# Linear attention and a gated MLP in one kernel: the products of keys with values in column halves of the array, each group kept together

## The chip, the cores and the metric

The kernel runs on one NeuronCore of a Trainium2 chip. A core has engines with queues of their own: TensorE (PE, with its weight loads shown apart as PEld), VectorE (DVE), ScalarE (ACT), GpSimd (POOL) and SyncE (SP), which starts the DMAs here. They meet only at semaphores. The metric is the device time of one execution in microseconds.

## The reference

Inputs are q, k, v of 8 batches x 8 heads x 576 positions x 64, a feature matrix w_phi (64 x 128), and the MoE's w_in (512 x 1024), conv_w (3 x 1024) and w_out (1024 x 512), which are float64 or float32.

```python
def phi(x):
    proj = np.einsum('bhsd,df->bhsf', x, w_phi)
    proj = proj - np.max(np.abs(proj), axis=-1, keepdims=True)
    return np.concatenate([np.exp(proj), np.exp(-proj)], axis=-1)
q_p, k_p = phi(q), phi(k)
kv = np.einsum('bhsf,bhsd->bhfd', k_p, v)
z = np.sum(k_p, axis=2)
num = np.einsum('bhsf,bhfd->bhsd', q_p, kv)
den = np.einsum('bhsf,bhf->bhs', q_p, z)[..., None] + 1e-06
x = num / den                                  # heads side by side: 8 x 576 x 512
h = np.maximum(x @ w_in, 0.0)
conv_out = conv_w[0]*h[t-1] + conv_w[1]*h[t] + conv_w[2]*h[t+1]   # along the sequence
out = (h * sigmoid(conv_out)) @ w_out
```

## The kernel before

**Tiling.** Four heads make a set (`qd`, two sets a batch). Of each set the 576 positions are worked on in five groups: group 0 holds the last 64 positions of all heads (n = 1), groups 1 to 4 hold 256 columns each (n = 2). `chains` lists the groups: the keys of batch 0, then by turns a query group of batch b and a key group of batch b + 1.

**A key group** (`k_process`, from line 222): DMAs bring kT and v, GpSimd splits k into a high and a low part (`kxh`, `kxl`), TensorE projects it with three products a tile (`kp`, lines 207 to 209), VectorE takes the largest absolute value and subtracts it (`km` line 214, `ks` line 216), ScalarE takes exp of both signs (`ke`, line 242: first s = 0, the positive sign, then s = 1), and TensorE multiplies these with v into the accumulators `kv` (two banks, i = 0 and 1; line 253 for group 0, line 258 for the others). v has a column of ones, so that z comes along: 65 columns, or 130 where two head pairs stand side by side (group 0). After group 4 ScalarE copies the accumulators to `kvf` (line 269).

**A query group** (`q_process`, from line 278) is projected in the same way (`qp`, `qm`, `qs`), transposed on TensorE (`tp`, line 298), exponentiated (`qe`, line 303), and multiplied with `kvf` into `nm` (line 322). These products stand in halves of the array: 64 stationary columns at a time, a = 0 and a = 64, which write partitions 0 to 63 and 64 to 127 of the result. VectorE divides (`dn`, `rc`, `x`, lines 333 to 336).

**The MoE** works on 12 tiles of 384 positions. `x_process` transposes x (`xt`, lines 376 and 379) and splits it (`xh`, `xl`); `h_part` makes 96 products for each tile and relu (`hp` line 407, `h` line 413); `conv_process` does the convolution, the sigmoid and the gate (`c`, `gh`, `gl`); `o_part` makes another 96 (`op`, line 468) and sends them out. `weight_process` loads and converts the MoE's weights at the start, mostly on VectorE (`w_t`, lines 101 to 108).

**What sets the order.** All these processes are generators. `merge` (line 553) keeps a clock of TensorE's time and steps through the first process that can run; `pe(n, ns)` adds n products to a count and ns to the clock, `wait` and `until` say when a process can go on, and `paced` (line 514, table `PACE`) says up to how many MoE products come before attention, by the count of attention products done. What is written so is then ordered for each engine by the framework's scheduler. `lead()` (line 505) raises the priority of what stands in it, so that it can pass MoE work that was written earlier; before the change it is around loads, VectorE's and ScalarE's steps, but not around TensorE's products. Within its limits the scheduler may spread a group's products among others.

```python
            elif can_m:
                if not step(moe, "m"):
                    moe = None
```

Of the kernel before, what the change touches and what calls it, by code (L numbers as in the profile page):

```python
# [24 lines left out]
VW = D + 1  # L25
# [4 lines left out]
ISSUE = 112  # L30
# [8 lines left out]

def PE_ORDER(tc):  # L40
    return nullcontext()


@with_exitstack
def kernel(
# [13 lines left out]
    nc = tc.nc  # L59
# [96 lines left out]
    now = [0.0]  # L156
    issued = [0.0]
    ready = {}

    def pe(n, ns):  # L160
        return ("pe", n, ns)

    def wait(ns):
        return ("wait", ns * LAT)

    def until(*keys):
        return ("until", [k for k in keys if k is not None])

    def set_ready(key, ns=0):
        ready[key] = now[0] + ns * LAT  # L170
# [8 lines left out]
    def load_split(src, b, qd, g, kind):  # L179
        c0, n = group_columns(g)  # L180
        if kind == "q" and 2 * b + qd < NQ_F32:
            raw = sb.tile([P, n * P], F32, name=f"{kind}r{b}_{qd}_{g}", tag="th", bufs=3)
            nc.sync.dma_start(out=raw, in_=src[b, qd, :, c0 : c0 + n * P])
            return n, raw, None
        raw = sb.tile([P, n * P], F32, name=f"{kind}r{b}_{qd}_{g}", tag="tr", bufs=3)
        nc.sync.dma_start(out=raw, in_=src[b, qd, :, c0 : c0 + n * P])
        hi = sb.tile([P, n * P], F32R, name=f"{kind}xh{b}_{qd}_{g}", tag="th", bufs=3)
        lo = sb.tile([P, n * P], F32R, name=f"{kind}xl{b}_{qd}_{g}", tag="tl", bufs=3)
        split(raw, hi, lo, nc.gpsimd, nc.gpsimd)
        return n, hi, lo  # L190
# [28 lines left out]
    kv = {}  # L219
    kvps = {}  # L220

    def k_process(b, qd, g):
        j = (b * NQ + qd) * 5 + g

        def back(key, k):
            return (key, j - k) if j >= k else None

        yield until(back("kp", 2), back("kv", 3))
        with lead():
            n, hi, lo = load_split(kT, b, qd, g, "k")  # L230
            v0 = 16 if g == 0 else 4 * (g - 1)
            v = sb.tile([P, 4 * VW], F32, name=f"v{b}_{qd}_{g}", tag="v", bufs=3)
            nc.sync.dma_start(out=v, in_=vt[b, qd, :, v0 * VW : (v0 + 4) * VW])
        yield wait(3000)
        yield until(back("kv", 2))
        set_ready(("kp", j))
        pr = yield from project(n, hi, lo, b, qd, g, "k")
        with lead():
            e = []
            for s in range(2):  # L240
                e.append(sb.tile([P, 2 * n, F], F32, name=f"ke{b}_{qd}_{g}_{s}", tag="ke", bufs=3))
                nc.scalar.activation(out=e[s], in_=pr, func=AF.Exp, scale=1.0 - 2.0 * s)  # L242
        yield wait(3000)
        yield until(back("kv", 1))
        if g == 0:
            kvps[b, qd] = [pk.tile([P, 2, 2 * VW], F32, name=f"kv{b}_{qd}_{i}", tag=f"kv{i}") for i in range(2)]
        kp = kvps[b, qd]
        for t in range(n):
            for i in range(2):
                for s in range(2):  # L250
                    lhsT = e[s][:, 2 * t + i, :]
                    if g == 0:
                        nc.tensor.matmul(out=kp[i][:, s, :], lhsT=lhsT, rhs=v[:, 2 * i * VW : 2 * (i + 1) * VW],  # L253
                                         start=(s == 0), stop=False, skip_group_check=True)
                        yield pe(2, 220)
                    else:
                        p0 = (g - 1) // 2 * VW
                        nc.tensor.matmul(out=kp[i][:, s, p0 : p0 + VW], lhsT=lhsT,  # L258
                                         rhs=v[:, (2 * t + i) * VW : (2 * t + i + 1) * VW],
                                         start=False, stop=(g % 2 == 0 and t == 1), skip_group_check=True)  # L260
                        yield pe(2, 112)
        if g == 4:

            yield until(("num", 10 * (b - 1) - 1) if b > 1 else None)
            r = []
            with lead():
                for i in range(2):
                    kf = sb.tile([P, 2, 2 * VW], F32, name=f"kvf{b}_{qd}_{i}", tag="kvf", bufs=8)
                    nc.scalar.activation(out=kf, in_=kp[i], func=AF.Copy)
                    r.append(kf)  # L270
            kv[b, qd] = r
            set_ready(("kvq", b, qd), 1500)
        set_ready(("kv", j))
# [4 lines left out]
    def q_process(b, qd, g):  # L278
        j = 10 * b + QORDER.index((qd, g))

        def back(key, k):
            return (key, j - k) if j >= k else None

        yield until(back("qp", 2))
        with lead():
            n, hi, lo = load_split(qT, b, qd, g, "q")
        yield wait(3000)
        yield until(back("tp", 2))
        set_ready(("qp", j))
        pr = yield from project(n, hi, lo, b, qd, g, "q")  # L290
        yield wait(1700)
        yield until(back("num", 2))
        set_ready(("tp", j))

        tp = pg.tile([P, 2, n, P], F32, name=f"tp{b}_{qd}_{g}", tag="g", bufs=4)
        for t in range(n):
            for i in range(2):
                nc.tensor.transpose(out=tp[:, i, t, :], in_=pr[:, 2 * t + i, :], identity=idn)  # L298
                yield pe(1, 60)
        with lead():  # L300
            qe = sb.tile([P, 2, 2, n, P], F32, name=f"qe{b}_{qd}_{g}", tag="qe", bufs=2)
            for s in range(2):
                nc.scalar.activation(out=qe[:, s], in_=tp, func=AF.Exp, scale=1.0 - 2.0 * s)  # L303
        yield wait(2000)
        yield until(back("num", 1), ("kvq", b, qd))

        if g > 0:
            xorder.append((b, g))
            i = len(xorder) - 1 - NX
            yield until(("xc", last_chunk(*xorder[i])) if i >= 0 else None)  # L310
        else:
            yield until(("xc", last_chunk(b - 2, 0)) if b > 1 else None)


        w = 2 * VW if g == 0 else VW
        p0 = 0 if g == 0 else (g - 1) // 2
        ps = pg.tile([P, n, 2, w], F32, name=f"nm{b}_{qd}_{g}", tag="g", bufs=4)
        for t in range(n):
            for i in range(2):
                for s in range(2):  # L320
                    for a in (0, 64):
                        nc.tensor.matmul(out=ps[a : a + 64, t, i, :], lhsT=qe[:, s, i, t, a : a + 64],  # L322
                                         rhs=kv[b, qd][i][:, s, p0 * VW : p0 * VW + w],
                                         start=(s == 0), stop=(s == 1))
        yield pe(16 * n, 100)
        parts = [(0, 64, 0), (64, 128, VW)] if g == 0 else [(0, P, 0)]
        with lead():
            dn = sb.tile([P, n, 2], F32, name=f"dn{b}_{qd}_{g}", tag="dn", bufs=4)
            rc = sb.tile([P, n, 2], F32, name=f"rc{b}_{qd}_{g}", tag="rc", bufs=4)
            x = sb.tile([P, n, 2, D], F32, name=f"x{b}_{qd}_{g}", tag="x0" if g == 0 else "x", bufs=4 if g == 0 else NX)  # L330
            xs[b, qd, g] = x
            for a, z, c0 in parts:
                nc.vector.tensor_scalar(out=dn[a:z], in0=ps[a:z, :, :, c0 + D], scalar1=1e-6, scalar2=None, op0=ALU.add)
            nc.vector.reciprocal(out=rc, in_=dn)
            for a, z, c0 in parts:
                nc.vector.tensor_tensor(out=x[a:z], in0=ps[a:z, :, :, c0 : c0 + D],
                                        in1=rc[a:z].unsqueeze(3).broadcast_to([z - a, n, 2, D]), op=ALU.mult)
        set_ready(("num", j))
        set_ready(("xs", b, qd, g), 1500)
# [165 lines left out]
    def lead():  # L505

        return tc.high_priority(offset=ahead[0])
# [17 lines left out]
    def step(p, kind):  # L525

        for what, *arg in p[1]:
            if what == "pe":
                n, ns = arg

                issued[0] = max(issued[0] + ISSUE * n, now[0] - 30 * ISSUE)
                now[0] = max(now[0], issued[0]) + ns
                done[kind] += n
                p[0] = now[0]
                return True
            if what == "wait":
                p[0] = now[0] + arg[0]
                return True
            p.append(arg[0])
            return True  # L540
        return False
# [43 lines left out]
    with PE_ORDER(tc):  # L585
        merge()
# [56 lines left out]
```

## Time and profile before

| | |
|---|---|
| Median of 3 runs | 858.72 us (856.85 to 863.38) |
| The profiled execution: its time | 853.69 us |
| Its span, first to last instruction | 851.9 us |
| Mean granted TensorE clock | 0.992 |
| Busiest after TensorE | VectorE, 537.3 us |

How to read what follows. A group row gives line, engine, operation, tiles out<-in, the part of the array used (rows*columns), the shape and the count; then busy time in us, the mean time of one in ns, and the idle time of the engine just before it with what ended that. A timeline row gives start, length, engine, line, operation, tiles and how many equal ones were merged. Matmuls overlap, so that one lasts longer than the distance to the next start; the distance is what one costs in a stream. A matmul with four-byte operands is shown as two records.

### The profile page before, as it was taken

To read this page: it belongs to the slowest core of one execution; us is meant where nothing else is said; L and a number is where in the kernel's file an instruction comes from. 1 tells how busy PE (TensorE), PEld (TensorE's weight loads), DVE (VectorE), ACT (ScalarE), POOL (GpSimd) and SP (SyncE) were. 2 spreads that over 40 slices of the span, in tenths; PEclk is the share of its full clock that TensorE was granted. 3 is DMA by queue.
4 is the path that set the end of the run, shared out by engine and by line. 5 is a ranking of instruction groups with operands and counts; after the bars stand their busy time and mean duration, and the time that the engine had idled before them with its cause. 6 is when DMAs were issued, how large, how long until landed. Compare 5 with 4: busy or idle time off the path is not lost.

```text
span 851.9 us, 17963 instructions
## 1 busy us (share of the span) xinstructions
PE 820.0 (96%) x7118; PEld 780.4 (92%) x7118; DVE 537.3 (63%) x1110; ACT 389.6 (46%) x678; POOL 275.0 (32%) x434
## 2 busy tenths in 40 slices
PE   7988898999999999998999999999999999999898
PEld 7887898999999999898998999999999999999798
DVE  7989978656565737655555665675564666574541
ACT  5676546354444344345344435425435434534332
POOL 5776853323322404213212421340332343110110
PEclk9999999999999999999999999999999999999899
DMA  6553311022012112012112201201201210000001
GB/s 196 178 157 125 104 36 42 22 76 61 25 54 67 44 35 73 20 48 72 33 44 60 67 19 63 63 17 57 70 17 47 76 50 29 22 3 28 10 28 47
DMA packets 46595, 48.74 MB, mean 57 GB/s; under 512 B 5296, under 2 KB 44464, under 8 KB 46512
## 3 DMA queue, kind: packets, MB, share of 16 engines
q1 hardware_dynamic: 46512, 47.59, 18.6%
q8 instruction: 57, 0.93, 0.5%
q14 instruction: 26, 0.21, 0.1%
HBM read 38.13 MB, written 9.44 MB: 56 GB/s over the span
## 4 chain that ended last, share of the span: by engine, by line
PE 83%; DVE 10%; ACT 3%; issue 2%; DMA 1%; POOL 0%; SPq 0%; ACTq 0%; POOLq 0%; DVEq 0%
PE hp L407 23%; PE op L468 23%; PE kv L258 10%; PE nm L322 9%; PE tp L298 3%; PE xt L376 3%; PE kp L207 2%; PE qp L207 2%; PE qp L209 2%; PE qp L208 1%; PE kp L208 1%; PE kp L209 1%; PE kv L253 1%; DVE ks L216 1%; DVE km L214 1%
## 5 line engine op out<-in xcount | busy, mean ns | idle before, releaser
L434 DVE SCALAR_TENSOR_TENSOR c<-h,cw,c 128x384 f32<-128x384 f32 (+3 forms) x256 | 131.3, 545 | 77.7 <-POOL c L428 75.8
L258 PE MATMUL kv<-v,ke 128*128 128x65 f32 x1024 | 131.0, 273 | 5.5 <-ACT ke L242 5.3
L258 PEld LDWEIGHTS kv<-v,ke 128*128 128x128 f32 x1024 | 126.3, 192 | 9.8 <-ACT ke L242 7.9
L242 ACT ACTIVATE ke<-ks 128x512 f32<-128x512 f32 (+1 forms) x160 | 87.2, 584 | 105.0 <-DVE ks L216 83.4
L407 PE MATMUL hp<-xh,win_hi 128*128 128x386 f32 x384 | 132.7, 356 | 2.0 <-ACT xh L69 1.7
L407 PE MATMUL hp<-xl,win_hi 128*128 128x386 f32 x384 | 132.3, 345 | 0.0
L407 PE MATMUL hp<-xh,win_lo 128*128 128x386 f32 x384 | 130.5, 340 | 0.0
L468 PE MATMUL op<-gh,wout_hi 128*128 128x384 f32 x384 | 129.7, 339 | 0.0
L468 PE MATMUL op<-gh,wout_lo 128*128 128x384 f32 x384 | 129.0, 336 | 0.0
L468 PE MATMUL op<-gl,wout_hi 128*128 128x384 f32 x384 | 128.9, 336 | 0.0
L428 POOL TENSOR_SCALAR c<-h,cw 128x384 f32<-128x384 f32 x96 | 58.4, 610 | 172.7 <-ACT h L413 172.7
L413 ACT ACTIVATE h<-hp 128x386 f32<-128x386 f32 x96 | 46.4, 493 | 140.1 <-PE hp L407 140.0
L322 PEld LDWEIGHTS nm<-kvf,qe 128*64 128x64 f32 x2304 | 84.2, 138 | 22.9 <-issue 12.9
L322 PE MATMUL nm<-kvf,qe 128*64 128x65 f32 (+1 forms) x2304 | 101.6, 234 | 3.8 <-ACT qe L303 2.1
L71 POOL TENSOR_SCALAR kxh<-kr 128x256 fp32r<-128x256 f32 (+1 forms) x80 | 35.8, 448 | 174.7 <-PE kp L208 141.5
L303 ACT ACTIVATE qe<-tp 128x512 f32<-128x512 f32 (+1 forms) x160 | 78.2, 555 | 25.5 <-PE tp L298 25.1
L74 DVE TENSOR_TENSOR gl<-c,gh 128x768 fp32r<-128x768 f32 x48 | 45.1, 964 | 61.3 <-ACT gh L69 61.2
L71 POOL TENSOR_SCALAR qxh<-qr 128x256 fp32r<-128x256 f32 (+1 forms) x70 | 30.8, 442 | 147.4 <-PE kp L208 77.0
L407 PEld LDWEIGHTS hp<-xh,win_hi 128*128 128x128 f32 x384 | 70.5, 188 | 4.9 <-ACT xh L69 2.2
L407 PEld LDWEIGHTS hp<-xl,win_hi 128*128 128x128 f32 x384 | 73.0, 190 | 0.4 <-issue 0.2
L407 PEld LDWEIGHTS hp<-xh,win_lo 128*128 128x128 f32 x384 | 72.6, 189 | 0.3 <-issue 0.2
L214 DVE TENSOR_REDUCE km<-kp 128x4 f32<-128x512 f32 (+1 forms) x80 | 50.3, 633 | 35.4 <-PE kp L209 34.6
(68 smaller groups left out, 1504.7 us busy)
## 6 DMA issues: line engine op xcount, KB each, us to landing
v<-in_vt_dram SPq DMA_DIRECT2D x80, 130.0 KB, 2.1
kr<-in_kT_dram SPq DMA_DIRECT2D x64, 128.0 KB, 2.1
qr<-in_qT_dram SPq DMA_DIRECT2D x64, 128.0 KB, 2.1
out_dram<-os SPq DMA_DIRECT2D x32, 192.0 KB, 1.9
w_r<-in_w_in_dram SPq DMA_DIRECT2D x8, 512.0 KB, 3.6
w_r<-in_w_out_dram SPq DMA_DIRECT2D x8, 512.0 KB, 3.4
out_dram<-os SPq DMA_DIRECT2D x32, 96.0 KB, 1.7
kr<-in_kT_dram SPq DMA_DIRECT2D x16, 64.0 KB, 2.1
```

Source lines behind the costliest of these rows:

```text
L71: nc.gpsimd.tensor_scalar(out=hi, in0=src, scalar1=1.0, scalar2=0.0, op0=ALU.mult, op1=ALU.add)
L74: eng_lo.tensor_tensor(out=lo, in0=src, in1=hi.bitcast(F32), op=ALU.subtract)
L214: nc.vector.tensor_reduce(out=m, in_=ps3, axis=AX, op=ALU.max, apply_absolute_value=True)
L242: nc.scalar.activation(out=e[s], in_=pr, func=AF.Exp, scale=1.0 - 2.0 * s)
L258: nc.tensor.matmul(out=kp[i][:, s, p0 : p0 + VW], lhsT=lhsT, rhs=v[:, (2 * t + i) * VW : (2 * t + i + 1) * VW], start=False, stop=(g % 2 = ...
L303: nc.scalar.activation(out=qe[:, s], in_=tp, func=AF.Exp, scale=1.0 - 2.0 * s)
L322: nc.tensor.matmul(out=ps[a : a + 64, t, i, :], lhsT=qe[:, s, i, t, a : a + 64], rhs=kv[b, qd][i][:, s, p0 * VW : p0 * VW + w], start=(s = ...
L407: nc.tensor.matmul(out=ps, lhsT=w_, rhs=x_[:, p, :], start=(k == 0), stop=(k == 11))
L413: nc.scalar.activation(out=hs, in_=ps, func=AF.Relu)
L428: nc.gpsimd.tensor_scalar(out=cv, in0=hs[:, o : o + TC], scalar1=cw[:, f, 1:2], scalar2=0.0, op0=ALU.mult, op1=ALU.add)
L434: nc.vector.scalar_tensor_tensor(out=cv[:, lo:hi], in0=hs[:, o + j - 1 + lo : o + j - 1 + hi], scalar=cw[:, f, j : j + 1], in1=cv[:, lo:hi ...
L468: nc.tensor.matmul(out=ps, lhsT=w_, rhs=x_, start=(i == 0), stop=(i == 23))
```

## The change

Three things are changed, all on TensorE. The products of keys with values are split into column halves like those of the queries: for each of them two products with 64 stationary columns, one for partitions 0 to 63 of the accumulator and one for 64 to 127, so 1152 instead of 576. Each group's products, of keys and of queries, stand in a block with raised priority (`lead()`) and in the order in which they are written (`PE_RUN`); both begin with s = 1, the exponential that is made last, and the outermost loop of the keys' block is now over s. And the planner is told of a group as one piece: 230 + 930 n ns, with no separate issue time.

```diff
+def PE_RUN(tc):
+    return tc.manual_schedule(engines={mybir.EngineType.PE})
...
-    def pe(n, ns):
-        return ("pe", n, ns)
+    def pe(n, ns, issue=ISSUE):
+        return ("pe", n, ns, issue)
...
-        for t in range(n):
-            for i in range(2):
-                for s in range(2):
-                    lhsT = e[s][:, 2 * t + i, :]
-                    if g == 0:
-                        nc.tensor.matmul(out=kp[i][:, s, :], lhsT=lhsT, rhs=v[:, 2 * i * VW : 2 * (i + 1) * VW],
-                                         start=(s == 0), stop=False, skip_group_check=True)
-                        yield pe(2, 220)
-                    else:
-                        p0 = (g - 1) // 2 * VW
-                        nc.tensor.matmul(out=kp[i][:, s, p0 : p0 + VW], lhsT=lhsT,
...
-                        yield pe(2, 112)
+        p0 = (g - 1) // 2 * VW
+        with lead(), PE_RUN(tc):
+            for s in (1, 0):
+                for t in range(n):
+                    for i in range(2):
+                        for a in (0, 64):
+                            lhsT = e[s][:, 2 * t + i, a : a + 64]
+                            if g == 0:
+                                nc.tensor.matmul(out=kp[i][a : a + 64, s, :], lhsT=lhsT,
+                                                 rhs=v[:, 2 * i * VW : 2 * (i + 1) * VW],
+                                                 start=(s == 1), stop=False, skip_group_check=True)
+                            else:
+                                nc.tensor.matmul(out=kp[i][a : a + 64, s, p0 : p0 + VW], lhsT=lhsT,
...
+        yield pe(16 * n, 230 + 930 * n, 0)
...
-        for t in range(n):
-            for i in range(2):
-                for s in range(2):
-                    for a in (0, 64):
...
-        yield pe(16 * n, 100)
+        with lead(), PE_RUN(tc):
+            for t in range(n):
+                for i in range(2):
+                    for s in (1, 0):
+                        for a in (0, 64):
...
+        yield pe(16 * n, 230 + 930 * n, 0)
...
-                issued[0] = max(issued[0] + ISSUE * n, now[0] - 30 * ISSUE)
+                issued[0] = max(issued[0] + issue * n, now[0] - 30 * ISSUE)
```

Two places show what this does to TensorE's order. The first is the third group of keys (`v_0_2`, set 0 of batch 3) about a third into the program. Names carry the set, the group and a running number; `ke_0_2_0` and `ke_0_2_1` are the two exponentials. Before:

```order
L258 MATMUL kv_0_0_3030<-v_0_2_3066,ke_0_2_0_3202 128x65
L258 MATMUL kv_0_1_3031<-v_0_2_3066,ke_0_2_0_3202 128x65
L207 MATMUL kp_0_4_3333<-wbd_hi,kxh_0_4_3237 128x256
L208 MATMUL kp_0_4_3333<-wbd_lo,kxh_0_4_3237 128x256
L209 MATMUL kp_0_4_3333<-wbd_hi,kxl_0_4_3238 128x256
L207 MATMUL kp_0_4_3333<-wbd_hi,kxh_0_4_3237 128x256
L208 MATMUL kp_0_4_3333<-wbd_lo,kxh_0_4_3237 128x256
L258 MATMUL kv_0_0_3030<-v_0_2_3066,ke_0_2_1_3204 128x65
L258 MATMUL kv_0_1_3031<-v_0_2_3066,ke_0_2_1_3204 128x65
L258 MATMUL kv_0_0_3030<-v_0_2_3066,ke_0_2_0_3202 128x65
```

The same group on TensorE after the change, with what stands on either side of it:

```order
L304 MATMUL tp_0_4_3641<-idn,qs_0_4_3523 128x128 x4
L383 MATMUL xt_0_3717<-idn,x_0_1_3061 128x128 x2
L264 MATMUL kv_0_0_3482<-v_0_2_3475,ke_0_2_1_3564 64x65 x2
L264 MATMUL kv_0_1_3483<-v_0_2_3475,ke_0_2_1_3564 64x65 x2
L264 MATMUL kv_0_0_3482<-v_0_2_3475,ke_0_2_1_3564 64x65 x2
L264 MATMUL kv_0_1_3483<-v_0_2_3475,ke_0_2_1_3564 64x65 x2
L264 MATMUL kv_0_0_3482<-v_0_2_3475,ke_0_2_0_3562 64x65 x2
L264 MATMUL kv_0_1_3483<-v_0_2_3475,ke_0_2_0_3562 64x65 x2
L264 MATMUL kv_0_0_3482<-v_0_2_3475,ke_0_2_0_3562 64x65 x2
L264 MATMUL kv_0_1_3483<-v_0_2_3475,ke_0_2_0_3562 64x65 x2
L211 MATMUL kp_0_4_3745<-wbd_hi,kxh_0_4_3635 128x256
```

The eight whole products, before cut in two by a projection, are sixteen halves in one piece, and those that read the later exponential come first.

The second place is on TensorE too, early in the program, where two query groups (`nm_1_1` and `nm_1_3`) meet the first key group of the next batch. Before:

```order
L253 MATMUL kv_0_0_753<-v_0_0_644,ke_0_0_0_717 128x130
L322 MATMUL nm_1_1_804<-kvf_1_0_749,qe_1_1_553 64x65 x4
L322 MATMUL nm_1_3_827<-kvf_1_0_749,qe_1_3_584 64x65 x4
L298 MATMUL tp_0_2_862<-idn,qs_0_2_651 128x128 x4
L253 MATMUL kv_0_0_753<-v_0_0_644,ke_0_0_1_719 128x130
L253 MATMUL kv_0_1_754<-v_0_0_644,ke_0_0_0_717 128x130
L253 MATMUL kv_0_1_754<-v_0_0_644,ke_0_0_1_719 128x130
L322 MATMUL nm_1_1_804<-kvf_1_1_751,qe_1_1_553 64x65 x4
```

After, at the same groups:

```order
L264 MATMUL kv_1_1_556<-v_1_4_734,ke_1_4_0_814 64x65 x2
L260 MATMUL kv_0_0_873<-v_0_0_742,ke_0_0_1_828 64x130 x2
L329 MATMUL nm_1_1_931<-kvf_1_0_869,qe_1_1_629 64x65
L329 MATMUL nm_1_3_957<-kvf_1_0_869,qe_1_3_660 64x65
L329 MATMUL nm_1_1_931<-kvf_1_0_869,qe_1_1_629 64x65
L329 MATMUL nm_1_3_957<-kvf_1_0_869,qe_1_3_660 64x65
```

Two groups whose blocks are open at the same time are interleaved product by product, where four of one group stood together before; and here kv and nm, both in halves now, follow each other directly.

More of the change, by code (lines that the diff above doesn't have):

```diff
@@ L247, in k_process @@
         kp = kvps[b, qd]
-        for t in range(n):
-            for i in range(2):
-                for s in range(2):
-                    lhsT = e[s][:, 2 * t + i, :]
-                    if g == 0:
-                        nc.tensor.matmul(out=kp[i][:, s, :], lhsT=lhsT, rhs=v[:, 2 * i * VW : 2 * (i + 1) * VW],
-                                         start=(s == 0), stop=False, skip_group_check=True)
-                        yield pe(2, 220)
-                    else:
-                        p0 = (g - 1) // 2 * VW
-                        nc.tensor.matmul(out=kp[i][:, s, p0 : p0 + VW], lhsT=lhsT,
-                                         rhs=v[:, (2 * t + i) * VW : (2 * t + i + 1) * VW],
-                                         start=False, stop=(g % 2 == 0 and t == 1), skip_group_check=True)
-                        yield pe(2, 112)
+        p0 = (g - 1) // 2 * VW
[11 more added lines that the diff above has]
+                                nc.tensor.matmul(out=kp[i][a : a + 64, s, p0 : p0 + VW], lhsT=lhsT,
+                                                 rhs=v[:, (2 * t + i) * VW : (2 * t + i + 1) * VW],
+                                                 start=False, stop=(g % 2 == 0 and t == 1), skip_group_check=True)
+        yield pe(16 * n, 230 + 930 * n, 0)
         if g == 4:
@@ L317, in q_process @@
         ps = pg.tile([P, n, 2, w], F32, name=f"nm{b}_{qd}_{g}", tag="g", bufs=4)
-        for t in range(n):
-            for i in range(2):
-                for s in range(2):
-                    for a in (0, 64):
-                        nc.tensor.matmul(out=ps[a : a + 64, t, i, :], lhsT=qe[:, s, i, t, a : a + 64],
-                                         rhs=kv[b, qd][i][:, s, p0 * VW : p0 * VW + w],
-                                         start=(s == 0), stop=(s == 1))
-        yield pe(16 * n, 100)
+        with lead(), PE_RUN(tc):
[3 more added lines that the diff above has]
+                        for a in (0, 64):
+                            nc.tensor.matmul(out=ps[a : a + 64, t, i, :], lhsT=qe[:, s, i, t, a : a + 64],
+                                             rhs=kv[b, qd][i][:, s, p0 * VW : p0 * VW + w],
+                                             start=(s == 1), stop=(s == 0))
+        yield pe(16 * n, 230 + 930 * n, 0)
         parts = [(0, 64, 0), (64, 128, VW)] if g == 0 else [(0, P, 0)]
@@ L528, in step @@
             if what == "pe":
-                n, ns = arg
-                issued[0] = max(issued[0] + ISSUE * n, now[0] - 30 * ISSUE)
+                n, ns, issue = arg
+                issued[0] = max(issued[0] + issue * n, now[0] - 30 * ISSUE)
                 now[0] = max(now[0], issued[0]) + ns
```

## The prediction

> **What bounds the kernel now.** I read the page first (busy time, chain), then the busy time by stage, then the groups by form, and last the timeline of TensorE around single runs of products, since the change alters how these follow each other.
>
> ```profile
> PE 820.0 (96%) x7118; PEld 780.4 (92%) x7118; DVE 537.3 (63%) x1110; ACT 389.6 (46%) x678; POOL 275.0 (32%) x434
> PE 83%; DVE 10%; ACT 3%; issue 2%; DMA 1%; POOL 0%; SPq 0%; ACTq 0%; POOLq 0%; DVEq 0%
> ```
>
> TensorE is busy for 96% of the span and holds 83% of the chain that ended last. The page's busy time overlaps from one matmul to the next, so I price TensorE's work by the distance between starts instead. By stage (columns: length, busy time and count of PE, PEld, DVE, ACT, POOL, granted clock, DMA share, GB/s):
>
> ```profile
> 0.00:20.00 20.00, 15.77 (x102) 14.37 (x102) 13.99 (x26) 10.45 (x20) 10.91 (x23) 1.00 0.63 196
> 20.00:100.00 80.00, 70.59 (x700) 63.83 (x699) 74.79 (x135) 52.33 (x100) 60.92 (x63) 0.96 0.48 149
> 100.00:160.00 60.00, 55.53 (x494) 52.37 (x493) 48.50 (x103) 29.19 (x51) 24.63 (x37) 1.00 0.12 34
> 160.00:750.00 590.00, 583.21 (x5235) 558.70 (x5233) 355.88 (x750) 263.38 (x456) 169.04 (x297) 1.00 0.16 48
> 750.00:852.00 102.00, 94.89 (x596) 91.13 (x596) 44.14 (x99) 34.26 (x53) 9.51 (x16) 0.97 0.07 24
> ```
>
> From 20 to 100 us VectorE is the bound, at 74.8 of 80 us: it prepares the weights beside the first batches. From 160 to 750 us TensorE is, at 583.2 of 590, and VectorE has 40% to spare. A shorter TensorE is paid in full in the long stage, and hardly before 100 us.
>
> The four groups that the change touches (mean of one | idle time before):
>
> ```profile
> L258 PE MATMUL kv<-v,ke 128*128 128x65 f32 x1024 | 131.0, 273 | 5.5 <-ACT ke L242 5.3
> L253 PE MATMUL kv<-v,ke 128*128 128x130 f32 x128 | 20.2, 290 | 1.0 <-ACT ke L242 1.0
> L322 PE MATMUL nm<-kvf,qe 128*64 128x65 f32 x2048 | 82.2, 227 | 1.7 <-DVE ks L216 1.2 <-DVE dn L333 0.5
> L322 PE MATMUL nm<-kvf,qe 128*64 128x130 f32 x256 | 19.3, 291 | 2.1 <-ACT qe L303 2.1
> ```
>
> A matmul of four-byte data shows as two records here (1024 for 512 products). kv stands on the whole array (128*128), nm already in column halves (128*64), with the same 65 and 130 moving columns. So nm is the price list for the new kv.
>
> **The price of a whole-array kv record.** On the timeline, a full group of sixteen between projections, and one of the eight that are 130 wide:
>
> ```profile
> 403.07 0.28 PE L209 MATMUL qp<-wbd_hi,qxl 128*128 128x256 f32 x1
> 403.19 1.89 PE L258 MATMUL kv<-v,ke 128*128 128x65 f32 x16
> 404.90 0.36 PE L207 MATMUL kp<-wbd_hi,kxh 128*128 128x256 f32 x1
> 405.10 0.28 PE L208 MATMUL kp<-wbd_lo,kxh 128*128 128x256 f32 x1
> ...
> 409.46 1.06 PE L253 MATMUL kv<-v,ke 128*128 128x130 f32 x8
> 410.36 0.60 PE L298 MATMUL tp<-idn,qs 128*128 128x128 f32 x4
> ```
>
> The next start is 1.71 us after the first kv, and the projection behind it takes 0.20 to its successor where 0.12 is usual: 1.79 us for 16, 112 ns a record. The wide ones take 0.90 / 8, also 112 ns: doubling the columns that stream costs nothing, so streaming is not what a record waits for. The sum before is 1152 x 112 ns = 129 us.
>
> **The price of a record in halves.** Two uninterrupted nm runs between matmuls of the MoE, one of 32 records and one of 16:
>
> ```profile
> 112.68 0.33 PE L407 MATMUL hp<-xh,win_lo 128*128 128x386 f32 x1
> 112.95 1.15 PE L322 MATMUL nm<-kvf,qe 128*64 128x65 f32 x32
> 114.03 0.44 PE L407 MATMUL hp<-xh,win_hi 128*128 128x386 f32 x1
> 114.31 0.34 PE L407 MATMUL hp<-xl,win_hi 128*128 128x386 f32 x1
> 114.49 0.34 PE L407 MATMUL hp<-xh,win_lo 128*128 128x386 f32 x1
> ...
> 418.36 0.33 PE L407 MATMUL hp<-xh,win_lo 128*128 128x386 f32 x1
> 418.62 0.69 PE L322 MATMUL nm<-kvf,qe 128*64 128x65 f32 x16
> 419.24 0.44 PE L407 MATMUL hp<-xh,win_hi 128*128 128x386 f32 x1
> 419.52 0.34 PE L407 MATMUL hp<-xl,win_hi 128*128 128x386 f32 x1
> ```
>
> First nm to the next hp: 1.08 us for 32, 0.62 for 16. The difference is 29 ns a record, 0.117 us for two halves with their four records. What is left is 0.62 - 16 x 0.029 = 0.15 us for each run, whatever its length. Going in costs another 0.09 (hp to nm 0.26 to 0.27, against 0.18 from hp to hp), coming out 0.10 (0.28 against 0.18). A run of column halves thus pays about 0.34 us once. Wide and lone products:
>
> ```profile
> 400.72 1.11 PE L322 MATMUL nm<-kvf,qe 128*64 128x130 f32 x16
> 401.76 0.87 PE L376 MATMUL xt<-idn,x 128*128 128x128 f32 x6
> ...
> 163.31 0.33 PE L322 MATMUL nm<-kvf,qe 128*64 128x65 f32 x2
> 163.57 0.39 PE L209 MATMUL qp<-wbd_hi,qxl 128*128 128x256 f32 x1
> ```
>
> Wide: (1.04 - 0.15) / 16 = 56 ns a record. A lone half, with no partner, takes 0.26 - 0.15 = 0.11 us, as long as a pair: the two halves run beside each other.
>
> **The change, part by part.**
> 1. kv in halves: 2048 narrow records x 29.2 ns = 59.8 us and 256 wide x 56 = 14.3, together 74 where 129 stood: -55 us. All of it comes from the narrow ones (114.7 to 59.8); the wide ones stay at 14.3. The ends of the range are the nm price (-55) and a lone half for each product (+12, worked out at the second rival); I take the first, since shape, weights and operand sizes are those of nm.
> 2. Runs of halves: counted in the orders, 108 stretches of nm before, 126 of nm and kv after (most of 16 or 32 products). At 0.34 us, and some 0.05 less where a transpose or (before) a kv follows: 35 before, 42 after, +7 us. So keeping groups together does not save runs; it keeps kv from paying 0.34 us for each scattered pair.
> 3. Mixed runs: where two groups interleave product by product (some 230 products, the second place shown), halves follow as first, first, second, second. If each pairs with its neighbour of the other half, only the ends lose, about 4 us for all; if none pairs, 230 x 0.05 = 12. I take 3, near the first, since a half can start as soon as its own columns are free, as the lone-half row suggests.
> 4. The first 100 us:
>
> ```profile
> 0.00:100.00 100.00, 30.48 (x239) 29.09 (x239) 0.97 0.51 158
> 0.00:100.00 100.00, 5.84 (x32) 5.16 (x32) 0.97 0.51 158
> ```
>
> Of the kv records 239 narrow and 32 wide (lines 258 and 253) fall there, where VectorE is the bound. VectorE's list up to the first convolution step is as long as before (164 instructions, 159 before). Up to 239 x 53 ns = 13 us of the 55 then come out as waiting for VectorE. Its 5 idle us of 80 leave room for some, so the loss lies between 0 and 13 and I take +7.
> 5. Order inside a group (negative exponential first, at the MoE's expense): one hazard is a run that starts before its second activation is done. Waits of TensorE by releaser:
>
> ```profile
> PE kv L258 <- ACT ke L242: 5.3, 6, 1.6
> PE tp L298 <- DVE qs L216: 4.7, 6, 1.2
> PE kp L207 <- POOL kxh L71: 4.1, 1, 4.1
> ```
>
> kv waits 5.3 us in six places. Starting with the later of the two exponentials makes a group wait once, ahead of it, not within. By the prices above the new order leaves a median 5.5 us of TensorE work between a K projection and its kv (5.1 before), so I set this at 0, between -5 and +10. Behind a waiting kv on TensorE stand MoE matmuls that could have run; that is what +10 stands for.
> 6. The planner's new costs and its count of attention products (kv counts double now, so the MoE's quota opens earlier) move MoE and attention against each other by some rows in a list otherwise alike. No DMA, activation or VectorE instruction is added or removed: 0, within 5 either way.
>
> Sum: -55 + 7 + 3 + 7 = -38 us on the profiled execution's 853.69, so 816 us. That execution lies 5.0 below the median shown (858.72); three runs spread over 6.5, so I add nothing for it.
>
> **Rivals.**
>
> ```profile
> L242 ACT ACTIVATE ke<-ks 128x512 f32<-128x512 f32 (+1 forms) x160 | 87.2, 584 | 105.0 <-DVE ks L216 83.4
> ```
>
> - *TensorE gets ahead of its suppliers.* With kv at half its time, a run meets exponentials that aren't there yet. An activation of ke takes 584 ns (the row above); if half of the 80 kv groups wait that long, 23 us of the gain go: 839. Against it: 40% spare on VectorE after 160 us and the distance in part 5. It takes all 80 to give the gain back.
> - *The halves of kv do not run beside each other.* Unlike nm, kv adds to two accumulators in turn over five groups. If each half goes alone, the narrow ones take 1024 x 0.11 = 113 us (115 before) and the wide 128 x 0.223 = 28.5 (0.223 is four records of 56 ns, a lone half taking as long as a pair; 14.4 before), with +7 for the runs: 853.7 + 12 + 7 = 873, slower. The point at which it decides: a pair must take under 2 x 0.112 - 10 / 576 = 0.207 us; nm takes 0.117. The Trainium skill ("TensorE: Matmul & The Clock Gate", LDWEIGHTS) puts a weight load at columns / 1.2 ns, which is 107 ns for 128 columns and 53 for 64; that fits the 112 ns here, and if the two loads of a pair stand in line the stream would save nothing, 861 us in all. The nm rows speak against that: four loads of 64 columns pass in 117 ns where the rule in line gives 213.
> - *The start is not lost and waits shrink* (part 4 at 0, part 5 at -5): 804.
>
> **How the numbers follow.** Forecast 0.65 (its own range 804 to 828), suppliers late 0.14 (828 to 845), no pairing 0.07 (861 to 873), better than 804 0.10, slower for other reasons (the order, a clash of buffers) 0.04. The range 800 to 838 leaves out the unpaired case, the worst of the late one and the best tail, about 2 in 10. A measurement of this kernel tells 1% (8.6 us) from no change: faster 0.86, same 0.05, slower 0.09.
>
> **What would show it.** kv should appear as 128*64 with 2048 and 256 records; a lone group of 32 between MoE matmuls should last 1.08 us to the next start, a mixed run 0.47 for each 16 more. Weight preparation should still hold VectorE above 90% from 20 to 100 us, and TensorE wait more there. From 160 us the same MoE tile should come earlier and earlier, by about 5 us per batch. I am wrong if a kv group takes 1.7 us or more, if TensorE's waits for ke reach tens of us, or if the end comes after 838.

## The result

| | before | changed | ratio, 95% interval |
|---|---|---|---|
| Median of 4 runs | 857.79 us | 832.35 us | 0.970 (0.964 to 0.976) |
| The profiled execution | 853.69 us | 833.15 us | |
| Its span | 851.9 us | 831.2 us | |
| Mean granted TensorE clock | 0.992 | 0.982 | |

The change makes the kernel faster by 25 us in the medians and 20.5 between the two profiled executions; 38 were forecast for those. Two executions below, one of experiment 7 (1487 us) and the profiled one of experiment 8 (1067 us, granted clock 0.654), are slow ones and stand in no time given. The profiled execution before is the shortest of that kernel on record: the other 35 take 854.97 to 863.70 us, and the 31 of them with a clock on record have 0.976 to 0.989, median 0.984. The page after, and the stages of the changed kernel in the columns used before:

```profile
PE 780.1 (94%) x8270; PEld 731.8 (88%) x8270; DVE 545.5 (66%) x1110; ACT 385.4 (46%) x676; POOL 277.4 (33%) x434
```

```profile
20.00:100.00 80.00, 60.78 (x864) 52.05 (x863) 74.12 (x131) 48.71 (x93) 57.81 (x58) 0.91 0.49 150
100.00:160.00 60.00, 54.04 (x667) 49.68 (x668) 50.31 (x101) 33.76 (x59) 28.71 (x40) 0.97 0.15 42
160.00:750.00 590.00, 573.48 (x6158) 542.61 (x6157) 374.59 (x789) 266.94 (x467) 174.82 (x303) 0.99 0.16 48
```

VectorE still holds 93% of the stretch from 20 to 100 us, while TensorE fell from 70.6 to 60.8 busy us there. In the long stage TensorE is busy for 573.5 of 590 us; before, it was 583.2, so it now stands still for 10 us more. The groups by form and a lone group of keys, in the early part of the program:

```profile
L264 PE MATMUL kv<-v,ke 128*64 128x65 f32 x2048 | 82.1, 228 | 6.9 <-ACT ke L246 6.8
L260 PE MATMUL kv<-v,ke 128*64 128x130 f32 x256 | 21.0, 293 | 3.2 <-ACT kvf L275 2.5 <-ACT ke L246 0.7
L329 PE MATMUL nm<-kvf,qe 128*64 128x65 f32 x2048 | 87.0, 229 | 13.4 <-DVE ks L220 5.7 <-ACT qe L309 3.9 <-DVE x L343 2.7
```

```profile
41.36 0.28 PE L213 MATMUL kp<-wbd_hi,kxl 128*128 128x256 f32 x1
41.57 1.15 PE L264 MATMUL kv<-v,ke 128*64 128x65 f32 x32
42.65 0.38 PE L211 MATMUL kp<-wbd_hi,kxh 128*128 128x256 f32 x1
42.87 0.28 PE L212 MATMUL kp<-wbd_lo,kxh 128*128 128x256 f32 x1
```

Thirty-two records of kv take 42.65 - 41.57 = 1.08 us, to the hundredth what nm took before. What grew is nm's idle time, 1.7 us before and 13.4 now. Its largest releaser is VectorE's subtraction `ks`, which nm does not read at all.

**Where the time went.** To compare whole runs I split each span into TensorE's priced work (every record at its distance in an undisturbed stream: 175 ns for hp, 174 op, 118 a projection, 109 a transpose, 112 a whole kv record, 29 or 56 a half, and the steps into and out of four-byte work and runs of halves; prices times counts, so not a measurement of its own) and lost time, which is the rest and includes stretches at half clock:

| us | priced work | lost by 100 us | lost by 150 us | lost after 150 us | span |
|---|---|---|---|---|---|
| before | 798.7 | 23.8 | 29.7 | 23.5 | 851.9 |
| changed | 750.6 | 37.9 | 46.9 | 33.7 | 831.2 |
| difference | -48.1 | +14.1 | +17.2 | +10.2 | -20.7 |

The work fell as forecast (-55 + 7 + 3 = -45). That the prices hold in the changed kernel is measured on its runs of halves: 112 of the 126 are undisturbed, and from their first record to the next start they last 146.7 us together where the prices give 145.6. The lost time grew by 27 where 7 was forecast; in the medians, which differ by 25.4, that is some 23, since the profiled execution before lost less time than is usual for it. All experiments ask where those 27 us come from, and whether the 48 belong to the halves or to the order. Each ran beside the kernel before, on the same chip.

### The profile page after: what moved, and what is told of

Its sections match the earlier page's. It is cut to its first block, busy times and chain, and to the rows that moved or that the text cites. A ratio compares the mean times of both kernels' runs of the same rounds, so it can differ in the third digit from the quotient of the medians.

```text
span 831.2 us, 20238 instructions
## 1 busy us (share of the span) xinstructions
PE 780.1 (94%) x8270; PEld 731.8 (88%) x8270; DVE 545.5 (66%) x1110; ACT 385.4 (46%) x676; POOL 277.4 (33%) x434
## 3 DMA queue, kind: packets, MB, share of 16 engines
q8 instruction: 66, 1.08, 0.5%
## 4 chain that ended last, share of the span: by engine, by line
PE 67%; DVE 7%; ACT 1%; issue 0%; ACTq 0%
PE op L475 21%; PE hp L414 20%; PE nm L329 7%; PE kv L264 6%; DVE gl L78 3%; PE tp L304 3%; PE xt L383 2%; PE qp L211 2%; PE qp L213 1%; PE qp L212 1%; PE kv L260 1%; DVE km L218 1%; PE kp L211 1%; DVE qm L218 1%; PE kp L213 1%; PE kp L212 1%
## 5 line engine op out<-in xcount | busy, mean ns | idle before, releaser
L441 DVE SCALAR_TENSOR_TENSOR c<-h,cw,c 128x191 f32<-128x191 f32 (+3 forms) x256 | 133.6, 555 | 71.9 <-POOL c L435 70.2
L329 PE MATMUL nm<-kvf,qe 128*64 128x65 f32 (+1 forms) x2304 | 104.3, 235 | 14.5 <-DVE ks L220 5.7
L435 POOL TENSOR_SCALAR c<-h,cw 128x384 f32<-128x384 f32 x96 | 61.2, 639 | 158.5 <-ACT h L420 158.5
L329 PEld LDWEIGHTS nm<-kvf,qe 128*64 128x64 f32 x2304 | 91.2, 141 | 26.0 <-issue 14.1
L78 DVE TENSOR_TENSOR gl<-c,gh 128x768 fp32r<-128x768 f32 x48 | 49.2, 1047 | 67.5 <-ACT gh L73 67.4
L264 PE MATMUL kv<-v,ke 128*64 128x65 f32 x2048 | 82.1, 228 | 6.9 <-ACT ke L246 6.8
L264 PEld LDWEIGHTS kv<-v,ke 128*64 128x64 f32 x2048 | 72.9, 141 | 17.4 <-ACT ke L246 8.1
L449 DVE TENSOR_TENSOR c<-c,h 128x384 f32<-128x384 f32 x96 | 49.8, 588 | 36.1 <-ACT c L445 36.1
```

Source lines behind the costliest of these rows:

```text
L78: eng_lo.tensor_tensor(out=lo, in0=src, in1=hi.bitcast(F32), op=ALU.subtract)
L264: nc.tensor.matmul(out=kp[i][a : a + 64, s, p0 : p0 + VW], lhsT=lhsT, rhs=v[:, (2 * t + i) * VW : (2 * t + i + 1) * VW], start=False, stop ...
L435: nc.gpsimd.tensor_scalar(out=cv, in0=hs[:, o : o + TC], scalar1=cw[:, f, 1:2], scalar2=0.0, op0=ALU.mult, op1=ALU.add)
L441: nc.vector.scalar_tensor_tensor(out=cv[:, lo:hi], in0=hs[:, o + j - 1 + lo : o + j - 1 + hi], scalar=cw[:, f, j : j + 1], in1=cv[:, lo:hi ...
L449: nc.vector.tensor_tensor(out=c4[:, f, :], in0=c4[:, f, :], in1=hs[:, o : o + TC], op=ALU.mult)
```

## The experiments

**1. Halves alone.** The kernel before, with kv in halves and nothing else.

```diff
-                    lhsT = e[s][:, 2 * t + i, :]
+                    for a in (0, 64):
+                        lhsT = e[s][:, 2 * t + i, a : a + 64]
...
```

> The kernel before with one edit: the products of keys with values in column halves; no block, no priority, the planner's entries as before. Theory A (the halves give the gain by their price on TensorE, the grouping only saves runs): counted in its order there are 206 runs of column halves instead of 126, 80 more at about 0.34 us, so some 20 to 27 us of the 55 are eaten; about 20 us faster than before, 832 to 846. Theory B (the gain comes from the order and the priority, the halves matter little): no faster than 1%, 850 or more.

Measured: 847.62 us beside 858.09, ratio 0.987 (0.984 to 0.990). It is faster by 10.5 us, half of what I expected and just outside my interval. Priced work is 776.9, 22 us below the kernel before and 26 above the changed one: the scattered runs eat what was expected. The rest of the miss is lost time. By 150 us it is 40.5, +10.8 against the kernel before, with no block or priority in it.

**2. Blocks alone.** The changed kernel, with kv on the whole array.

```diff
-                        for a in (0, 64):
-                            lhsT = e[s][:, 2 * t + i, a : a + 64]
+                        lhsT = e[s][:, 2 * t + i, :]
...
```

> The changed kernel with whole-array products of keys and values; blocks, priority, planner's costs and counts as in the change. Theory A: TensorE's priced work is that of before within 5 us and the waits of the changed order stay, so the same as before or slower, 850 to 872. Theory B: nearly all of the gain is here, 830 to 840.

Measured: 875.69 us, ratio 1.020 (1.015 to 1.025): slower, by 17.6 us, and 4 us above theory A's interval. Theory B falls. Work 797.4, as before; lost by 150 us 35.9 (+6.2), after it 35.9 (+12.4). The waits of TensorE after 150 us in this kernel name the same pair as in the changed one:

```profile
PE nm L327 <- DVE ks L220: 8.6, 3, 2.9
PE qp L211 <- DVE ks L220: 3.5, 2, 1.7
PE kp L211 <- DVE dn L338: 1.7, 1, 1.7
```

So the blocks by themselves cost time through waits, and pay only with the halves, whose runs they join: halves alone gain 10.5 us, blocks alone lose 17.6, and both together gain 25.

**3. No priority.** The changed kernel, both blocks without `lead()`.

```diff
-        with lead(), PE_RUN(tc):
+        with PE_RUN(tc):
```

> The changed kernel without the raised priority of both blocks; halves, written order and planner's costs stay. Counted in its order: 208 runs of halves instead of 126. Theory A: 82 more runs at 0.34 us cost 24 to 28 us, less some waits that the priority made: 845 to 858. Rival C (the priority itself makes TensorE wait, and this is what is missing from the forecast): 832 or less.

Measured: 847.74 us, ratio 0.986 (0.982 to 0.990), as theory A has it; rival C falls. Work 777.9, 27 us above the changed kernel's; lost after 150 us 27.2 against 33.7, and by 150 us 41.8 against 46.9. The priority is what keeps the runs of halves whole; it saves 27 us of work and costs some 12 of lost time, 6 of them after 150 us.

**4. The count of the keys' products as before.**

```diff
-        yield pe(16 * n, 230 + 930 * n, 0)
+        yield pe(8 * n, 230 + 930 * n, 0)
         if g == 4:
```

> The changed kernel with the keys' products counted as before (8 n instead of 16 n for each group), so that the MoE's quota opens no earlier than before; nothing else. Theory D (the quota lets the MoE run ahead, attention then stands alone and TensorE waits, which is the missing part of the gain): 818 to 826. Theory A alone: 115 runs instead of 126, 4 us less work, 825 to 834.

Measured: 832.79 us, ratio 0.970 (0.966 to 0.974), the changed kernel's own. Theory D falls: the MoE's quota is not where the gain went. The order has 115 runs, as counted, but the 4 us less work brought no time.

**5 and 6. The start without the weights' arithmetic.** Both kernels with this edit:

```diff
-        float64_round(raw, w, tmp[:, 1, :])
+        low = raw.rearrange("p (n two) -> p n two", two=2)[:, :, 0]
+        nc.scalar.activation(out=w, in_=low.bitcast(U32), func=AF.Copy, scale=2.0**-38)
```

> The kernel before with VectorE's share of the weight preparation left out (the float64 weights of the MoE are not rebuilt; one ScalarE conversion of their low words stands in, so the output is not the reference's): three VectorE and one GpSimd instruction fewer for each of 16 pieces. The bound of the first 100 us goes. Theory A (VectorE binds the start): TensorE's lost time up to 100 us, 24 us in the kernel before, falls to 8 to 16: 840 to 852.

> The changed kernel with the same work left out. Theory A: what the column halves save before 100 us is no longer given back to VectorE, so this one gains more than the kernel before does: lost time up to 100 us falls from 38 to 20 or less, 808 to 818, and the distance between the two kernels grows from 25 to 30 to 40 us. Rival E (the start is lost to the blocks and their priority, not to VectorE): the distance stays at 22 to 28 us.

Measured: 846.63 and 813.27 us beside 858.64, ratios 0.987 (0.985 to 0.989) and 0.947 (0.945 to 0.950). The distance between the two kernels is 33.4 us instead of some 25 to 26: theory A in the main, with a remainder for rival E. The stretch from 20 to 100 us, first the kernel before with this edit, then the changed one with it:

```profile
20.00:100.00 80.00, 77.38 (x781) 73.26 (x782) 43.98 (x96) 47.51 (x94) 40.07 (x56) 0.94 0.48 147
...
20.00:100.00 80.00, 69.30 (x1026) 62.35 (x1023) 44.13 (x100) 48.54 (x97) 39.52 (x53) 0.96 0.47 147
```

VectorE falls from 74 to 44 busy us, and the changed kernel puts 1026 records into the 80 us instead of 864. Lost by 150 us is now 20.9 and 28.6; by 100 us the changed kernel still loses about 25, where 20 or less was expected. Of the 17.2 us that the change lost in the start, 9.5 went with the weights' arithmetic; 7.7 stay with it out of the way. The edit takes out four VectorE instructions for each of 16 pieces (1110 before, 1046 after; the expectation says three), one of GpSimd and, net, one of ScalarE, so VectorE's own share is not separated from theirs. Experiments 1 and 2 split the same 17.2 us another way: halves alone lost 10.8 in the start and blocks alone 6.2. So 7.7 fits the blocks, but what they wait for there was not taken apart.

**7. Priority for the keys' blocks only.** nm's block without `lead()`.

> The changed kernel with the raised priority on the keys' blocks alone, not on those of the queries (nm). Counted in its order: 159 runs of halves instead of 126, 11 us more work on TensorE. Theory F (raised nm blocks stand where no accumulator bank is free, and TensorE waits there for VectorE, 2.9 us at 258, 456 and 652 us): these three waits and the half clock behind them go, 10 to 15 us less lost time after 150 us, so 828 to 836. Rival: the waits stay, 840 to 848.

Measured: 851.0 us, ratio 0.991 (0.988 to 0.994), slower than both expectations. The three waits are gone, but others took their place (1.8 us of xt behind `qe` and 1.6 of kp behind `kxh`, three times each, and one of 2.7 of qp behind `qe`), and lost time after 150 us is 40 instead of 34. Theory F is half right: the three waits go with nm's priority, but taking the priority away doesn't win.

**The place itself.** The changed kernel around 257 us, TensorE first, then VectorE:

```profile
255.43 0.28 PE L213 MATMUL kp<-wbd_hi,kxl 128*128 128x256 f32 x1
258.59 1.87 PE L329 MATMUL nm<-kvf,qe 128*64 128x65 f32 x32 [2.88 <-DVE ks L220]
260.39 1.11 PE L304 MATMUL tp<-idn,qs 128*128 128x128 f32 x4
261.30 0.63 PE L383 MATMUL xt<-idn,x 128*128 128x128 f32 x2
...
456.09 1.47 PE L329 MATMUL nm<-kvf,qe 128*64 128x65 f32 x32 [2.86 <-DVE ks L220]
...
652.09 2.00 PE L329 MATMUL nm<-kvf,qe 128*64 128x65 f32 x32 [2.70 <-DVE x L343]
```

```profile
252.65 1.37 DVE L78 TENSOR_TENSOR gl<-c,gh 128x768 fp32r<-128x768 f32 x1
253.94 0.68 DVE L220 TENSOR_TENSOR qs<-qp,qm 128x512 f32<-128x512 f32 x1
254.54 1.37 DVE L78 TENSOR_TENSOR gl<-c,gh 128x768 fp32r<-128x768 f32 x1
...
256.59 0.66 DVE L218 TENSOR_REDUCE km<-kp 128x4 f32<-128x512 f32 x1
257.17 0.68 DVE L218 TENSOR_REDUCE qm<-qp 128x4 f32<-128x512 f32 x1
257.77 0.68 DVE L220 TENSOR_TENSOR ks<-kp,km 128x512 f32<-128x512 f32 x1
```

The results of kp, qp, tp, nm and xt share four accumulator banks (the pool `pg`). nm stands right behind two projections of keys and has to wait for a bank; the `ks` that ends at 258.45 us has read one out. That it is the bank follows from the code and from nm not reading `ks`; no run had more banks. VectorE comes to it late because two subtractions of gl (1.37 us each) stand ahead. The wait returns at 456.1 us (2.86) and 652.1 us (2.70): once in two batches, about 197 us apart. At the third the profile names `x`, the last step of VectorE's division, which reads an older nm out of the same pool. It is paid twice, as the windows of the wait, the time behind it, and the time after show (the third number from the right is the granted clock):

```profile
255.71:258.59 2.88, 0.00 (x1) 0.03 (x1) 2.88 (x8) 0.11 (x1) 1.92 (x4) 1.00 0.23 68
258.80:262.10 3.30, 3.30 (x42) 2.85 (x40) 1.94 (x5) 1.91 (x5) 0.00 (x0) 0.50 0.09 24
262.20:265.00 2.80, 2.80 (x66) 2.60 (x64) 0.69 (x2) 1.55 (x3) 0.67 (x2) 1.00 0.18 48
```

After 2.88 us without a matmul TensorE is granted half its clock for more than 3 us, and the 32 nm records take 260.39 - 258.59 = 1.80 us instead of 1.08. In the 50 us around each place 5.3 to 5.8 us are lost, 16.6 for the three. The kernel before lost 5.0 in the same three windows.

**8 and 9. Half of gl on GpSimd.** The changed kernel, run twice; the rows and windows here are of the second.

```diff
-            split(c4[:, f : f + 2, :], gh4[:, a : a + 2, :], gl4[:, a : a + 2, :], nc.scalar, nc.vector)
+            split(c4[:, f : f + 2, :], gh4[:, a : a + 2, :], gl4[:, a : a + 2, :], nc.scalar,
+                  nc.vector if a == 0 else nc.gpsimd)
```

> The changed kernel with every second pair of gl (the low part of the gate, 1.37 us each on VectorE at the place of the wait) on GpSimd. Theory G (the three waits are VectorE's backlog behind gl): each becomes 1 to 2 us shorter and the half clock behind it goes in part, 822 to 829. Rival (the bank is what is short, whatever VectorE does): 830 to 836.

> The kernel with half of gl on GpSimd once more, for a trace at the granted clock that the others have. Theory G: 818 to 822; after 150 us the three waits of nm (2.9 us each in the changed kernel) are under 1.5 us each, no half-clock stretch follows them, and the lost time after 150 us falls from 34 to 20 to 24 us.

Measured: 818.77 us beside 858.64, ratio 0.954 (0.952 to 0.956), and 819.69 beside 859.36, 0.954 (0.950 to 0.957): 13 us faster than the change. The same place, on TensorE:

```profile
255.64 0.28 PE L213 MATMUL kp<-wbd_hi,kxl 128*128 128x256 f32 x1
255.84 1.15 PE L329 MATMUL nm<-kvf,qe 128*64 128x65 f32 x32
257.99 0.63 PE L304 MATMUL tp<-idn,qs 128*128 128x128 f32 x4 [0.99 <-DVE ks L220]
```

nm starts 0.20 us behind the projection and lasts 1.15 us, as a run of 32 does at full clock; a wait of 0.99 is left for the transpose, and no half clock follows. Lost after 150 us falls from 33.7 to 19.6, below the kernel before; lost by 150 us stays at 46.9. In the three windows of 50 us it falls from 16.6 to about 7. Theory G holds; the first run and the lost time came out a little better than its intervals.

**10. The same edit in the kernel before.**

> The kernel before with half of gl on GpSimd. Theory G (VectorE's backlog behind gl became a wait only through the change): the kernel before has no such three waits, so at most 5 us: 853 to 860. Rival (moving gl helps any kernel by as much): 842 to 848.

Measured: 854.99 us, ratio 0.994 (0.992 to 0.997), as theory G has it. It helps by 4.4 us there and by 13 in the changed kernel, so about two thirds are the cure of waits that the change made.

**11. All of gl on GpSimd.** `nc.gpsimd` in both cases.

> The changed kernel with all of gl on GpSimd, where one takes about 1.9 us against 0.96 on VectorE. Theory G: VectorE's backlog at the place is gone altogether, but four in a row take 7.5 us before the output products may begin, where there is cover: 814 to 822. Rival (GpSimd becomes late for the products): 824 or more.

Measured: 823.34 us, ratio 0.957 (0.953 to 0.961), between theory and rival, and no better than half. Two new waits of 2.1 and 0.6 us stand near 200 us.

**12. Half of gl on GpSimd, and another cost in the planner.** `yield pe(16 * n, 1160, 0)` for both kinds of group.

> The kernel with half of gl on GpSimd, and the planner told 1.16 us for every group (the trace has 1.28 for the narrow ones) instead of 2.09 for those with n = 2. In its order 112 runs of halves stand instead of 125. By the price on TensorE it has 4.6 us less work: 812 to 818. Rival (a planner that believes TensorE faster puts queries' products closer behind their transposes, down to 1.1 us, and the waits take back more than the work gives): 820 to 830.

Measured: 830.38 us, ratio 0.968 (0.964 to 0.972); the expected 812 to 818 fails and the rival holds, at the very end of its interval. Work is 745.5, 4.6 us less as counted, but lost time is 83.5 against 66.5: nm waits 1.5 us for its exponentials at three places and 2.5 at a fourth, and the start loses 6 us more. A truer number in the planner made a worse order.

## Why the prediction was right, and which terms were mis-sized

- *Price of kv in halves (part 1).* Right, and shown: 1.08 us for 32 records, the two halves beside each other. The second rival falls, and with it the reading of the Trainium skill ("TensorE: Matmul & The Clock Gate", LDWEIGHTS) in which the loads of a pair stand in line.
- *Runs (part 2) and mixed runs (part 3).* Right: the traces have the 108 and 126 runs. A mixed run loses 0.05 us once: fifteen undisturbed runs of 64 records in which kv and nm alternate last 2.07 us each, whatever the number of changes, and runs of 64 with one change or none 2.02. The price of a run holds for short ones too: in experiments 1 and 3 the undisturbed runs last 3% longer than the prices give. At that price their 206 and 208 runs instead of 126 are 26 and 27 us more work; in time they are 15 us slower than the changed kernel, because they lose some 12 us less in waits.
- *The first 100 us (part 4).* The mechanism was right and the size wrong. I allowed 0 to 13 and took 7; by 100 us 14.1 us went, by 150 us 17.2. VectorE's "5 idle us of 80", in which I let faster products fit, stayed idle (74.1 busy after, 74.8 before). Experiments 5 and 6 put 9.5 of the 17.2 on the weights' arithmetic. The other 7.7 I had no term for; experiment 2 points to the blocks, and what they wait for stays open.
- *Waits of TensorE (part 5).* I set 0 within -5 and +10; it was +10.2, at the edge. I looked for waits for exponentials (6.8 us for the narrow kv, against 5.3) and not for accumulator banks: a block moved forward needs a free bank as much as its inputs, and the distances that I counted said nothing of that. The half clock behind such a wait was in no term.
- *The first rival* (TensorE ahead of its suppliers) came true in part, at nm and through banks rather than at kv. Its price, up to 23 us for late exponentials, was near the 20 by which the lost time passed the forecast, but that is chance: half of those 20 were lost in the start, and the waits later were mostly for banks. "About 5 us per batch" in the long stage came out nearer to 4.5: the first op product starts 9 us later than before (170.7 against 161.6 us), and the end comes 21 us earlier, 30 us over nearly seven batches.
- *The base of the sum.* I took 38 us off the profiled execution and added nothing for its lying below the median. From the median of 857.79 the same 38 us give 820, so 4 of the 16 us between 816 and 832.35 are this term.
- The measured 832.35 lies inside the range of 800 to 838, but outside the forecast's own 804 to 828: it is within the interval that the first rival had, and that rival's width is what made the range hold.

## What to carry to other kernels

Products with few moving columns (65 here) and four-byte weights can run as two column halves beside each other at half the price, but each unbroken run of halves costs a fixed 0.34 us here: keep them together, and count the runs in the order before building it. Work that is raised in priority must be checked for the output bank it needs, and for who frees it, as well as for its inputs. A few microseconds of TensorE idle can cost nearly as much again in half clock (8.4 us of waits at the three places, and 13.6 us at half clock behind them), so a short backlog on another engine is worth removing even when that engine is one-third idle.

## What the runs showed of the hardware that was not expected

- All three waits of 2.7 to 2.9 us in the changed kernel's long stage had half clock behind them, but the length of a wait does not decide it alone. In the kernel of experiment 2 nm goes on at full clock at 267.93 us after a wait of 2.85 us, and a wait of only 1.75 us, which ends at 404.61 us, has half clock behind it. The windows behind these two:

```profile
268.00:271.40 3.40, 3.40 (x54) 3.33 (x54) 1.98 (x6) 3.15 (x6) 0.00 (x0) 1.00 0.07 19
406.10:409.50 3.40, 3.40 (x36) 3.06 (x32) 1.95 (x4) 1.06 (x3) 1.41 (x3) 0.50 0.25 76
```

The Trainium skill ("TensorE: Matmul & The Clock Gate", Part 1) names about 3.4 us of idle as the limit and windows of that length; the length fits the windows above, the limit is lower here.
- The mean clock does not tell the two kernels apart. In the profiled executions it makes 2 x 0.018 x 831 = 30 us at half clock against 14 before, but at the usual 0.984 of the kernel before it is 27. The profiled execution with half of gl moved has 0.991, its three others 0.983 to 0.985. What the change added is seen at the three places, not in the mean.
- A whole-array kv record cost 112 ns whether 65 or 130 columns streamed, and a record of a half that streams 130 cost 56, with twice as many records: for these the halves brought nothing.
- gl took 1.37 us on VectorE at the place shown and 0.96 at another, and GpSimd's second `kxh` there took 1.11 us where 0.41 is usual. In these rows the one that starts later is the one that gets longer: gl at 252.65 us starts inside `kxl` (252.47 to 253.21), and `kxh` at 253.17 inside that gl (to 254.02). GpSimd in the changed kernel there:

```profile
251.97 0.41 POOL L75 TENSOR_SCALAR kxh<-kr 128x256 fp32r<-128x256 f32 x1 [17.64 <-PE qp L212]
252.47 0.74 POOL L78 TENSOR_TENSOR kxl<-kr,kxh 128x256 fp32r<-128x256 f32 x1
253.17 1.11 POOL L75 TENSOR_SCALAR kxh<-kr 128x256 fp32r<-128x256 f32 x1
```

And the first gl in the kernel of experiment 9, with GpSimd idle until 251.07 us:

```profile
250.28 0.96 DVE L78 TENSOR_TENSOR gl<-c,gh 128x768 fp32r<-128x768 f32 x1 [6.46 <-ACT gh L73]
```

Both fit what the Trainium skill ("GPSIMD Engine Reference", Specifications) says of the SBUF interfaces that the two engines share; no experiment changed which of the two starts first. The two gl at the place are 0.8 us of VectorE's backlog longer for it.
